# A local-attention and gated-product kernel: weight parts split in fewer passes, and another order for the head

## The chip, the cores and the metric

One core of one Trainium2 chip runs the whole kernel. The metric is device time in microseconds, from the launch's first work to its last. Engines are called PE (TensorE), DVE (VectorE), ACT (ScalarE), POOL (GpSimd) and SP (SyncE, which here only issues transfers).

## The reference, cut to what matters

Batch 4, 8 heads, 768 tokens, head size 64. A query attends to the tokens less than 16 away and to 24 block summaries (of keys the maximum over 32 tokens, of values the mean). The attention's output, 3072 tokens by 512, goes through two weight matrices of 512 by 1536, whose results are multiplied, and a third of 1536 by 512.

```
k_sum = k.reshape(B, H, nb, 32, D).max(axis=3);  v_sum = v.reshape(B, H, nb, 32, D).mean(axis=3)
scores_l = where(|i - j| < 16, scale * q @ k.T, -1e9);  scores_s = scale * q @ k_sum.T + log(32)
a = softmax(concat(scores_l, scores_s));  x = a @ concat(v, v_sum)
a = x @ w_a;  b = x @ w_b;  out = (a * b) @ w_out
```

The weights reach the kernel as numbers of 64 bits, two 32-bit words each.

## The kernel before, in words

**Tiles.** A tile is 128 tokens of a batch, all heads. Chunks `u` are of two tiles in batch 0 and three in the others. The scores of a tile are 120 columns for each of four head pairs and two halves `h` (96 neighbouring keys and 24 summaries), 480 columns for a half, in one PSUM bank.

**The first two chunks** (tiles 0 to 3 of batch 0, `first_attention`) have code of their own. `first_keys` loads six blocks of 128 keys (one token a partition, a run of 256 bytes for each head), turns each with four PE transposes (L507), copies it in two pieces to `kT` (L565, L566, ACT) and takes the block maxima (L573, DVE). A query tile is loaded and turned in the same way (L507), and ACT copies it with the factor 0.125 (L973). In `scores`, PE first writes the mask into the bank, as two parts in the reduced format fp32r multiplied by an identity (L695), and adds the 32 passes of scores (L708). DVE takes the maximum (L745) from the bank, ACT the exponentials with their sums (L759), DVE adds 1e-9 (L768), takes the reciprocal (L779) and makes from it diagonal matrices (L786). `transposes` multiplies by these (L807), which divides and transposes in one step; ACT copies the result (L819). `values` multiplies by the values (L856), after which ACT (L876) and DVE (L880) split the result in a high and a low part, `x`. The values of a tile come by `load_values` in three pieces, and the block means by six blocks of two tokens a partition, a POOL addition (L1000) and twelve PE passes (L991). Later chunks put the mask on with a DVE pass (L737) and divide on POOL (L794).

**Weights.** The three matrices are cut in 36 parts of 524 KB (a, b and o for each of 12 blocks `f`; part `i` is 0 to 35 in the order a0, b0, o0, a1, ...). `load_part` brings one, `convert(j)` splits parts 2j and 2j+1 in a high and a low part in fp32r. For a half (one part) ACT rescales the high words into bank `c0` (L424), DVE shifts (L432), DVE masks the exponent into bank `c1` (L439), DVE multiplies the low words by it (L445); ACT rounds to the high part (L477), POOL subtracts it (L482) and adds the low words' share (L488). From j = 3 on, the last steps take both halves at once. Loads for j > 3 wait until `convert(j - 4)` has read its words.

**The expert matmuls.** An item is a chunk (or both first chunks) with a block `f`: `up` (L1110, 12 matmuls for a and 12 for b), ACT and DVE make the product and split it (L1184 to L1192, L1214 to L1222), `down` (L1232). An item of one of the first chunks needs that chunk's `x` of both tiles, and the high and low words of its parts.

**What sets the order.** Every operation is added to a list (`Work`) with its engine, a rank, an estimated duration, and what it reads and writes. `emit` issues them engine by engine; for as long as `ORDER` has numbers for an engine, that engine's instructions come in exactly this order (a number is the place in the list). Each engine works through its instructions in order, so one that waits holds up all behind it; this holds for the transfers that SP issues. `SPIN` are matmuls without use that keep PE busy in the first 40 us.

## Time and profile before

| what | us |
|---|---|
| median of 3 runs (658.7 to 659.53) | 659.19 |
| span of the profiled execution, first to last instruction | 656.9 |
| median less that span | 2.3 |
| busy: PE / DVE / ACT / POOL | 647.7 / 409.9 / 250.8 / 187.8 |
| first expert matmul (L1110) starts | 38.33 |

The profiled execution has no time of its own beside its span; the difference to the runs' median stands for what lies around it. In the lists of instructions a row has start, length of the run of equal instructions, engine, line, operation, output and inputs, count, and in brackets idle time and what ended it. "PE" rows are matmuls, whose ends are modelled; "PEld" are weight loads. A plain fp32 matmul is two rows, one for each pass.

### The profile page before, as it was taken

The numbers are of one execution on the slowest core, as the hardware profiler recorded it, in microseconds if no ns is written. First come the engines' busy times: TensorE is split into PE (matmuls) and PEld (weight loads), VectorE is DVE, ScalarE is ACT, GpSimd is POOL, SyncE is SP. The second block draws the span as 40 slices with busy tenths as digits, with TensorE's granted clock in tenths as the row PEclk, the third lists the DMA queues.
The fourth block names the chain that finished last, engine by engine and source line by source line (L and its number), as shares of the span: only waits on it lengthen the run. The fifth ranks groups of instructions, "written<-read, shape, count | busy, mean of one in ns | idle before, by whom it ended". The sixth has DMA issues, their size and how long they took to land.

```text
span 656.9 us, 12984 instructions
## 1 busy us (share of the span) xinstructions
PE 647.7 (99%) x4943; PEld 599.3 (91%) x4943; DVE 409.9 (62%) x857; ACT 250.8 (38%) x749; POOL 187.8 (29%) x246
## 2 busy tenths in 40 slices
PE   8899999999999999999999999999999999999997
PEld 6699888899989999999999999999999999999997
DVE  3899999997786784666767846667652531122212
ACT  4997676523443441433333313343321411121111
POOL 6498999847333440111010101110100100000000
PEclk9999999999999999999999999999999999999999
DMA  9998666353443443322112422221100200010001
GB/s 218 277 286 243 229 188 173 79 118 105 128 92 78 112 95 57 71 82 44 39 39 52 84 42 43 41 82 35 25 1 1 71 1 1 0 49 1 0 1 49
DMA packets 158198, 54.71 MB, mean 83 GB/s; under 512 B 135736, under 2 KB 151352, under 8 KB 158136
## 3 DMA queue, kind: packets, MB, share of 16 engines
q1 hardware_dynamic: 157992, 53.75, 33.9%
q8 instruction: 39, 0.64, 0.4%
q14 instruction: 23, 0.19, 0.1%
q10 hardware_dynamic: 144, 0.13, 0.1%
HBM read 47.41 MB, written 6.44 MB: 82 GB/s over the span
## 4 chain that ended last, share of the span: by engine, by line
PE 89%; DMA 6%; SPq 2%; ACT 1%; issue 1%; POOL 0%; DVE 0%; DVEq 0%
PE h L1110 54%; PE o L1232 27%; PE c L708 3%; PE o L856 3%; SPq L357 2%; DMA raw<-in_moe_w_out_dram 1%; DMA space<-in_v_dram 1%; DMA raw<-in_moe_w_b_dram 1%; DMA raw<-in_moe_w_a_dram 1%; DMA space<-in_q_dram 1%; DMA qin<-in_q_dram 1%; SPq L389 1%; PE c L1110 1%; POOL space L482 0%; PE c L856 0%
## 5 line engine op out<-in xcount | busy, mean ns | idle before, releaser
L1110 PE MATMUL h<-x,w 128*128 128x384 f32 (+2 forms) x2064 | 389.1, 321 | 0.0
L1110 PEld LDWEIGHTS h<-x,w 128*128 128x128 f32 x2064 | 331.3, 190 | 10.5 <-issue 0.6
L1232 PE MATMUL o<-w,gh 128*128 128x512 f32 x534 | 131.7, 382 | 0.0
L1217 DVE TENSOR_TENSOR h<-h,g 128x384 f32<-128x384 f32 x71 | 40.2, 566 | 136.4 <-PE h L1110 128.8
L1219 ACT CAST gh<-h 128x384 fp32r<-128x384 f32 x71 | 34.0, 478 | 204.6 <-DVE h L1217 202.0
L1232 PEld LDWEIGHTS o<-w,gh 128*128 128x128 f32 x534 | 97.6, 189 | 12.2 <-issue 1.6
L840 DVE STREAM_TRANSPOSE pt<-s 32x256 f32<-32x256 f32 x228 | 99.4, 436 | 13.0 <-POOL s L794 8.3
L794 POOL TENSOR_TENSOR s<-s,nml 128x480 f32<-128x480 f32 x40 | 39.4, 987 | 220.2 <-DVE nml L779 218.1
L1110 PE MATMUL h<-late,w 128*128 128x384 f32 x288 | 93.9, 326 | 0.0
L759 ACT ACTIVATE s<-s,nml 128x120 f32<-128x120 f32 x160 | 61.3, 386 | 38.0 <-DVE nml L745 37.8
L1232 PE MATMUL o<-w,gl 128*128 128x512 f32 x231 | 63.3, 381 | 0.0
L1110 PEld LDWEIGHTS h<-late,w 128*128 128x128 f32 x288 | 54.4, 189 | 0.9
L1222 DVE TENSOR_TENSOR gl<-h,gh 128x384 fp32r<-128x384 f32 x71 | 39.4, 555 | 23.0 <-ACT gh L1219 22.5
L1214 ACT COPY g<-h 128x384 f32<-128x384 f32 x71 | 34.0, 478 | 51.3 <-PE h L1110 50.9
L1232 PEld LDWEIGHTS o<-w,gl 128*128 128x128 f32 x231 | 43.3, 189 | 6.5 <-issue 0.5
L639 POOL TENSOR_TENSOR S<-S 96x256 f32<-96x256 f32 (+3 forms) x58 | 33.0, 571 | 43.8 <-DMA S<-in_v_dram 41.1
L737 DVE SCALAR_TENSOR_TENSOR s<-c,mask 128x480 f32<-128x480 f32 x40 | 25.8, 652 | 24.0 <-PE c L708 23.9
L424 ACT ACTIVATE c<-raw 128x512 f32<-128x512 f32 x36 | 29.3, 814 | 13.2 <-DVE S L432 5.7
L759 ACT ACTIVATION_READ_ACCUMULATOR s<-s,nml 128x1 f32 x160 | 30.2, 189 | 0.0
L482 POOL TENSOR_TENSOR space<-space,w 128x1024 f32<-128x1024 f32 (+1 forms) x14 | 26.7, 1912 | 3.5 <-ACT w L477 3.2
L488 POOL TENSOR_TENSOR w<-space 128x1024 fp32r<-128x1024 f32 (+1 forms) x14 | 26.7, 1912 | 0.9
L745 DVE TENSOR_REDUCE nml<-s 128x4 f32<-128x480 f32 x40 | 25.8, 648 | 0.7
(139 smaller groups left out, 586.0 us busy)
## 6 DMA issues: line engine op xcount, KB each, us to landing
raw<-in_moe_w_a_dram SPq DMA_DIRECT2D x12, 512.0 KB, 5.7
raw<-in_moe_w_b_dram SPq DMA_DIRECT2D x12, 512.0 KB, 7.9
raw<-in_moe_w_out_dram SPq DMA_DIRECT2D x12, 512.0 KB, 4.8
out_dram<-S SPq DMA_DIRECT2D x23, 256.0 KB, 2.2
qin<-in_q_dram SPq DMA_DIRECT2D x288, 16.0 KB, 1.7
S<-in_v_dram SPq DMA_DIRECT2D x24, 192.0 KB, 3.3
kin<-in_k_dram SPq DMA_DIRECT2D x38, 100.0 KB, 2.5
vw<-in_v_dram SPq DMA_DIRECT2D x18, 192.0 KB, 3.4
```

The costliest lines, as they stand in the source:

```text
L424: nc.scalar.activation(bank["c0"], high[:, :, 1].bitcast(F32), AF.Prelu, scale=2.0**-112, alpha=-(2.0**32))
L482: lambda ms=ms, f8=f8: nc.gpsimd.tensor_tensor(out=f8, in0=f8, in1=parted(0)[:, ms].bitcast(F32), op=ALU.subtract),
L639: lambda: nc.gpsimd.tensor_tensor(out=out, in0=i0, in1=i1, op=ALU.add),
L759: lambda h=h, c=c, sums=sums: nc.scalar.activation(s[h][:, c, :], x[h][:, c, :], AF.Exp, bias=m[:, 0, h, c : c + 1], scale=1.0, accum_out= ...
L794: lambda h=h, r=r: nc.gpsimd.tensor_tensor(out=s[h], in0=s[h], in1=r[:, :, None].broadcast_to([P, NP, KN]), op=ALU.mult,),
L840: lambda js=js, qs=qs, rs=rs: nc.vector.transpose(out=pv[js, rs, qs], in_=sv[qs, rs, js]),
L1110: nc.tensor.matmul(ps, w[:, c, part, :], (xt[:, 4 * xpart : 4 * xpart + 4] if both else inputs_of(u, xpart))[:, :, c].rearrange("p g (a b) ...
L1214: act(CHAIN, 0.13 + W / 1030, [ak], gk, lambda: nc.scalar.copy(out=g, in_=pa))
L1217: lambda: nc.vector.tensor_tensor(out=pb, in0=pb, in1=g, op=ALU.mult),
L1219: act(CHAIN, 0.16 + W / 1030, [bk], [ghk], lambda: nc.scalar.copy(out=gh, in_=pb))
L1222: lambda: nc.vector.tensor_tensor(out=gl, in0=pb, in1=gh.bitcast(F32), op=ALU.subtract),
L1232: nc.tensor.matmul(bank[ok[j]], (gh if first else gl)[:, j * P : (j + 1) * P], w[:, :, part, :].rearrange("p (z a) n -> p z n a", a=2), st ...
```

## The change

*Weights.* A half takes one pass of ACT (rescaled high words, straight to SBUF), one of DVE for the low words (`tail`: times 2^-29, at most 7, as an integer into bank `c0` or `c1` by half), and one of DVE (`join`: shift by 3 and or). The product has the low bits in place, so that POOL's one subtraction gives the low part. For j < 3 each half has tiles of its own.

```
-            bank["c0"], high[:, :, 1].bitcast(F32), AF.Prelu, scale=2.0**-112, alpha=-(2.0**32)
...
-                    out=f.bitcast(I32), in0=e.bitcast(I32), scalar1=3, scalar2=None,
-                    op0=ALU.logical_shift_left,
...
-                    out=s.bitcast(I32), in0=f.bitcast(I32), scalar1=-(1 << 23), scalar2=None,
-                    op0=ALU.bitwise_and,
...
-                    out=p, in0=low.bitcast(U32), scalar=2.0**-52, in1=s, op0=ALU.mult, op1=ALU.mult
+            def scale(f=f, words=words):
+                nc.scalar.activation(
+                    f, words()[:, :, 1].bitcast(F32), AF.Prelu, scale=2.0**-112, alpha=-(2.0**32)
+                )
+            def tail(t=t, words=words):
+                nc.vector.tensor_scalar(
+                    out=t, in0=words()[:, :, 0].bitcast(U32), scalar1=2.0**-29, scalar2=7.0,
+                    op0=ALU.mult, op1=ALU.min,
+                )
+            def join(f=f, t=t):
+                nc.vector.scalar_tensor_tensor(
+                    out=f.bitcast(I32), in0=f.bitcast(I32), scalar=3, in1=t,
+                    op0=ALU.logical_shift_left, op1=ALU.bitwise_or,
+                )
...
             pool(
-                rank + 0.1 * hs[0], takes, hi, f,
...
-                    out=f8, in0=f8, in1=parted(0)[:, ms].bitcast(F32), op=ALU.subtract
...
-                    out=parted(1)[:, ms], in0=f8, in1=p8, op=ALU.add
+                rank + 0.1 * hs[0], 0.2 + 1.1 * len(hs), hi + f, lo,
+                lambda hs=hs, f8=f8: nc.gpsimd.tensor_tensor(
+                    out=parted(1, hs), in0=f8, in1=parted(0, hs).bitcast(F32), op=ALU.subtract
+                ),
             )
```

*Keys and queries of the first chunks.* A load takes four heads and 256 tokens, two tokens a partition (runs of 512 bytes); still six loads of keys and four of queries, of 262 KB each. Eight matmuls of 64 columns of weights by the identity turn one, the halves `h` into the two column halves of PE. ACT's copies pick the tokens up alternately; the queries of a chunk are turned together (`turn_queries`) and copied in four half pieces without the factor. The key maxima wait for PE alone.

```
+    def paired(x):
+        return x.rearrange("h (p t) d -> p h (t d)", t=2)
+    def turn_pairs(bk, x):
+        v4 = x.rearrange("p (h t d) -> p h t d", t=2, d=D)
+        for c in range(2):
+            for t in range(2):
+                n = 2 * c + t
+                for h in range(2):
+                    nc.tensor.matmul(
+                        bank[bk][h * D : (h + 1) * D, n * P : (n + 1) * P],
+                        v4[:, 2 * c + h, t, :], ident, start=True, stop=True,
+                        tile_position=(0, h * D),
+                    )
```

*Masks and division.* The mask matmuls and the three POOL instructions that make their inputs go. The first chunks have the DVE pass that the others have, and DVE multiplies by the reciprocal before four plain transposes.

```
-        if masked:
-            pe(rank + 0.1, 0.96, MK, banks, masks)
...
-                    lambda h=h, r=r, d=d: nc.vector.tensor_tensor(
-                        out=d[:, h], in0=ident[:, None, :].broadcast_to([P, NP, P]),
-                        in1=r[:, :, None].broadcast_to([P, NP, P]), op=ALU.mult,
+                    lambda h=h, r=r: nc.vector.tensor_tensor(
+                        out=s[h], in0=s[h], in1=r[:, :, None].broadcast_to([P, NP, KN]),
+                        op=ALU.mult,
...
-                    nc.tensor.matmul(
-                        bank[banks[h]][:KN, c * P : (c + 1) * P], s[h][:, c, :KN], d[:, h, c, :],
-                        start=True, stop=True,
+                    nc.tensor.transpose(
+                        bank[banks[h]][:KN, c * P : (c + 1) * P], s[h][:, c, :KN], ident
                     )
```

*Order.* `ORDER` and the banks of `SPIN` are new (its sixteen sizes are the same), and `ORDER` now ends about where the first two chunks' items end; behind that, ranks decide. Ranks of the first weight loads and value loads are earlier. The beginnings, with the numbers translated:

- SP: key blocks 1, 0, 2, 3, query half 1, key blocks 5, 4, query half 0; part 1; the six value blocks; two pieces of tile 0's values; part 0; their third piece; part 3; the queries of tiles 2 and 3; part 2; tile 1's values; part 4; a piece of tile 2's values; part 5; another; part 11; two pieces of values; part 7; values; part 9; values; parts 6, 13, 12, 8, 15, 10. (Before: eight loads; part 0; three value blocks, a query load; part 1; ...; tile 0's values behind part 5.)
- PE: five `SPIN`; turns of key blocks 1, 0, 2, 3, query half 1, keys 5, 4, query half 0, with one `SPIN` between; two `SPIN`; scores of tile 0; two; scores of tile 1; the means; two; transposes and product of tile 0; half of tile 1's transposes; the second queries; scores of tile 2; the other half; three `SPIN`; product of tile 1; scores of tile 3; the `up` of items 0 and 1; transposes and products of tiles 2 and 3; one `SPIN`; the `down` of item 0. (Before: scores of tiles 2 and 3 and six halves of transposes stand ahead of the first `up`, with the products of tiles 0 and 1 behind the scores of tile 3.)
- ACT: copies of key blocks 0, 2, 1, 5, a query quarter, 3, 4, two quarters; scale of part 1; a quarter; round part 1; exponentials of tile 0 and of half of tile 1; two copies of means; two copies of transposes; one exponential; scales of parts 0 and 3; split of tile 0; the other exponentials of tile 1; ...
- DVE: six key maxima; tail and join of part 1; masks and maxima of tile 0, of half of tile 1; divisions between; tail of part 0, tail and join of part 3; ...

More of the change, by code (lines that the diff above doesn't have):

```diff
@@ L383, in fn @@
         def fn():
-            if j not in raws:
-                raws[j] = wp.tile([P, 2048], I32, tag=f"W{j}", name=f"raw{j}")
-            dst = raws[j][:, i % 2 * 1024 : (i % 2 + 1) * 1024]
+            dst = raw(i)
             if nm != "o":
@@ L449, in convert @@
-        for n, h in [(n, h) for h in range(2) for n in range(3)]:
-            f, p, e, s, r = [fk[h]], [pk[h]], ["c0"], ["c1"], [rk[h]]
-            if n == 0:
-                act(CHAIN, 0.52, r, e, lambda h=h: scale(h))
-            reads, writes = ((e, f), (f, s), (r + s, p + [f"done{j}"] + r))[n]
-            dve(rank, 0.6, reads, writes, lambda n=n, h=h: step(n, h))
-        def parted(part):
-            if j not in homes:
-                homes[j] = wp.tile([P, 8, 2, P], F32R, tag=f"W{j}", name=f"w{j}")
-            return homes[j][:, :, part, :]
+        whole = [f"whole{j}"] if single and j > 2 else []
@@ new lines, in convert @@
+        for h in range(2):
+            f, t = fx[h], bank[f"c{h}"].bitcast(I32)
+            words = lambda h=h: raw(2 * j + h).rearrange("p (n t) -> p n t", t=2)
+            def scale(f=f, words=words):
[12 more added lines that the diff above has]
+                )
+            act(rank - 0.05, 0.66, [rk[h]], [fk[h], f"whole{j}.{h}"], scale)
+            dve(rank, 0.6, [rk[h]], [f"c{h}", f"done{j}.{h}"], tail)
+            dve(rank, 0.6, [f"c{h}"], [fk[h]], join)
@@ L461, in convert, with parted @@
+        work.add("-", 0, 0, 0, [f"done{j}.{h}" for h in range(2)], [f"done{j}"], lambda: None)
+        if whole:
+            work.add(
+                "-", 0, 0, 0, [f"{x}{j}.{h}" for x in ("whole", "done") for h in range(2)], whole, lambda: None
+            )
+        def parted(part, hs):
+            y = home(2 * j + hs[0])
+            if len(hs) == 2:
+                y = both[j]
+            return y[:, :, part, :]
         for hs in spans:
-            ms = slice(4 * hs[0], 4 * (hs[-1] + 1))
@@ L687, in scores @@
         m, mk = nml[t % 2], f"nml{t % 2}"
-        masked = u < FILL
-        def masks():
-            for h in range(2):
-                for part in range(2):
-                    nc.tensor.matmul(
-                        bank[banks[h]].rearrange("p (c x) -> p c x", x=P)[:, :, :KN], identr,
-                        maskr[part][:, kind, None, :KN].broadcast_to([P, NP, KN]),
-                        start=(part == 0), stop=False,
-                    )
+        first = u < FILL
         def fn():
@@ L728, in scores @@
         s = [t[:, :, :KN] for t in s]
[L729 to L730 removed]
+        x, xk = s, sk
         for h in range(2):
@@ L733, in scores @@
                 rank = rank_of(u, t) - 0.1 + 0.02 * h
[L734 to L742 removed]
+            dve(
+                rank, 0.6, [banks[h]], [sk[h], *(f"{sk[h]}{c}" for c in range(NP) if first)],
+                lambda h=h: nc.vector.scalar_tensor_tensor(
+                    out=s[h], in0=y[h],
+                    scalar=0.125, in1=mask[:, kind, None, :KN].broadcast_to([P, NP, KN]),
+                    op0=ALU.mult, op1=ALU.add,
+                ),
+            )
             dve(
@@ L752, in scores @@
             l = m[:, 1, h, :]
-            sums, r = l, x[h][:, :, 0] if masked else l
+            sums, r = l, y[h][:, :, 0] if first else l
             for c in range(NP):
@@ L902, in first_attention @@
         first_keys()
-        for takes, fn in (
-            (0.3, lambda: nc.gpsimd.tensor_copy(out=identr, in_=ident)),
-            (0.45, lambda: nc.gpsimd.tensor_copy(out=maskr[0], in_=mask[:, :2, :])),
-            (0.6, lambda: nc.gpsimd.tensor_tensor(
-                out=maskr[1], in0=mask[:, :2, :], in1=maskr[0].bitcast(F32), op=ALU.subtract
-            )),
-        ):
-            pool(-1, takes, [], MK, fn)
         q0, qk = spot(3)
```

266 lines of the change are left out of this document (119 added, 147 removed), and 54 rows, old and new, of the table ORDER.

## The prediction

> **What bounds the kernel now.** I read the page first, then TensorE's (PE) instructions in order of time, then the groups by line, then stretches of time for the transfers. The page:
>
> ```profile
> span 656.9 us, 12984 instructions
> PE 647.7 (99%) x4943; PEld 599.3 (91%) x4943; DVE 409.9 (62%) x857; ACT 250.8 (38%) x749; POOL 187.8 (29%) x246
> ...
> PE   8899999999999999999999999999999999999997
> ```
>
> The instructions of PE in order of time (start, length of the run of equal instructions):
>
> ```profile
> 1.43 2.50 PE L1338 MATMUL h<-ident 128*128 128x512 f32 x4 [1.43 <-POOL ident masks.py:199]
> 4.03 1.12 PE L507 MATMUL o<-ident,space 128*128 128x128 f32 x4
> ...
> 6.61 1.09 PE L507 MATMUL c<-ident,space 128*128 128x128 f32 x4
> 7.50 1.13 PE L1338 MATMUL h<-ident 128*128 128x256 f32 x4
> ...
> 9.78 0.60 PE L507 MATMUL c<-ident,space 128*128 128x128 f32 x4
> 10.21 0.64 PE L507 MATMUL o<-ident,space 128*128 128x128 f32 x4
> ...
> 12.73 0.60 PE L507 MATMUL h<-ident,space 128*128 128x128 f32 x4
> 13.10 1.12 PE L695 MATMUL o<-space 128*128 128x480 f32 x4
> 14.14 1.05 PE L708 MATMUL o<-kT,qT 64*64 64x120 f32 x32
> 15.01 1.00 PE L708 MATMUL o<-kT,space 64*64 64x120 f32 x32
> ...
> 34.09 1.15 PE L856 MATMUL h<-pt,vw 120*64 120x64 f32 x32
> 35.07 1.10 PE L856 MATMUL h<-space,space 120*64 120x64 f32 x32
> 36.40 1.98 PE L807 MATMUL o<-pt,s 128*120 128x128 f32 x16 [0.23 <-DVE pt L786]
> 38.33 2.92 PE L1110 MATMUL h<-x,w 128*128 128x256 f32 x24
> 41.09 1.04 PE L807 MATMUL o<-space,space 128*120 128x128 f32 x8
> ...
> 47.89 1.15 PE L856 MATMUL o<-space,space 120*64 120x64 f32 x32
> 48.98 0.70 PE L1232 MATMUL o<-w,gl 128*128 128x512 f32 x2
> ```
>
> The stretch from 80 to 100 us (columns: stretch, its length, busy time and instructions of PE, weight loads, VectorE, ScalarE, GpSimd, then clock, DMA, GB/s):
>
> ```profile
> 80.00:100.00 20.00, 20.00 (x94) 17.51 (x93) 19.19 (x33) 15.53 (x28) 19.09 (x10) 1.00 0.58 156
> ```
>
> From 38.33 PE never waits noticeably: 94 matmuls of 512 columns in 20 us are 0.213 us each, which is the rate at which the columns stream, and that in a stretch where VectorE and GpSimd are 95% busy. So what the change saves on those two is worth nothing by itself there. The time is: the point at which the expert matmuls (L1110) start, plus work that the change leaves alone. Only the head, up to about 49 us, can pay. In it PE waits for a chain through ScalarE (ACT), VectorE (DVE) and the loads.
>
> **The parts, with their prices.** Groups by line (count, then busy time and mean ns of one):
>
> ```profile
> L759 ACT ACTIVATE s<-s,nml 128x120 f32<-128x120 f32 x160 | 61.3, 386 | 38.0 <-DVE nml L745 37.8
> L737 DVE SCALAR_TENSOR_TENSOR s<-c,mask 128x480 f32<-128x480 f32 x40 | 25.8, 652 | 24.0 <-PE c L708 23.9
> L745 DVE TENSOR_REDUCE nml<-o 128x4 f32<-128x480 f32 x8 | 4.9, 646 | 0.0
> L432 DVE TENSOR_SCALAR space<-c 128x512 int32<-128x512 int32 x22 | 15.0, 682 | 2.6 <-ACT c L424 2.6
> L439 DVE TENSOR_SCALAR c<-space 128x512 int32<-128x512 int32 x22 | 15.1, 684 | 0.2
> L445 DVE SCALAR_TENSOR_TENSOR space<-raw,c 128x512 f32<-128x512 uint32 x22 | 16.8, 762 | 0.1
> L424 ACT ACTIVATE c<-raw 128x512 f32<-128x512 f32 x36 | 29.3, 814 | 13.2 <-DVE S L432 5.7 <-DVE space L432 4.2 <-DVE s L737 3.0
> L482 POOL TENSOR_TENSOR space<-space,w 128x1024 f32<-128x1024 f32 (+1 forms) x14 | 26.7, 1912 | 3.5 <-ACT w L477 3.2
> L786 DVE TENSOR_TENSOR space<-ident,o 128x512 f32<-128x512 f32 x4 | 2.7, 678 | 0.0
> L768 DVE TENSOR_SCALAR o<-nml 128x4 f32<-128x4 f32 x8 | 1.2, 159 | 1.6 <-ACT s L759 1.3 <-ACT space L759 0.3
> L477 ACT CAST w<-space 128x512 fp32r<-128x512 f32 x6 | 3.7, 630 | 0.0
> L819 ACT COPY space<-o 120x512 f32<-120x512 f32 x4 | 2.4, 597 | 0.5 <-PE o L807 0.5
> ```
>
> *Weights.* A half part loses one of three DVE passes (L432, L439, L445: 0.68+0.68+0.76 = 2.13 us) and one of two GpSimd passes (L482 and its like). Neither new pass is in the trace. The tail pass reads the same strided words as L445 and the join reads SBUF and PSUM at once as L445 does: between 0.68 (L439) and 0.81 (ScalarE's strided pass L424), I take 0.76 for both. 36 halves save 36 x (2.13-1.52) = 22 us of DVE (20 to 28 by the bounds), all under PE's cover after 38 us. In the head, six halves save 4 us on an engine that is full there.
>
> *Masks.* 16 mask matmuls (four at 13.10 end where scores start at 14.14: about 1 us a tile) leave PE. DVE gets eight passes of 0.65 (L737), and its eight diagonal builds (L786, 0.68) become eight divisions of like size. Maxima and exponentials stay, so the head's DVE gains 5.2 us and loses 4: it is no lighter, only the order differs. The scale of 0.125 moves from the query copies into the mask pass, at no instruction; the key maxima no longer wait for the key copies, which frees an engine that has nothing else to do then.
>
> *Transposes.* Scaled ones are eight matmul passes of about 0.11 us a half tile (16 in the 1.93 us from 36.40 to 38.33), plain ones four (10.21 less 9.78: 0.43 us). The paired turns are 16 passes of 64 columns of weights. If the two halves of the columns run side by side, as in L856 (32 passes from 34.09 to 35.07, 0.031 each, against 0.055 for 64 columns one after another), a turn costs 16 x 0.054 = 0.87 against 0.43 now.
>
> *Loads.* Stretches with 256-byte runs only, with mostly 512-byte runs, and with mostly 1 KB runs (the last column counts):
>
> ```profile
> 6.00:9.00 3.00, 2.63 (x13) 2.17 (x11) 1.27 (x2) 1.85 (x6) 2.40 (x14) 1.00 1.35 218
> 14.00:15.00 1.00, 1.00 (x33) 0.86 (x36) 0.06 (x1) 0.64 (x1) 0.00 (x0) 1.00 1.23 291
> 23.00:25.00 2.00, 2.00 (x17) 1.72 (x17) 1.65 (x6) 1.63 (x7) 0.94 (x2) 1.00 1.10 347
> 30.00:35.00 5.00, 4.13 (x73) 3.06 (x73) 4.96 (x12) 4.95 (x22) 4.86 (x5) 1.00 0.74 154
> ```
>
> Two tokens a partition make runs of 512 bytes: 262 KB take 0.90 us and not 1.20. The first key comes at about 3.7 (4.03 less 0.3), the eighth load at 10.0, where the last query was turned at 12.73 before. With the new order of SP behind it, at these rates: part 1 at 11.6 (524 KB at 347: 1.5), the six value blocks by 17.6, tile 0's values (360 KB in 256-byte runs) at 20.8 behind part 0, the second queries at 24 behind part 3, tile 1's values (393 KB) at 27.3 behind part 2, part 4 at 28.9.
>
> **The walk through the head**, each engine in its written order. Five warm-up matmuls of 1,024 columns together stand where 640 took 2.50: PE is free at about 5.1. The first turn is at half rate (four transposes from 6.61 to 7.50 are 0.22 each, those from 9.78 to 10.21 0.11), 1.8; the second straddles the release near 7.5 and ends at 8.2. ScalarE then paces:
>
> ```profile
> 7.74 0.42 ACT L565 COPY kT<-c 128x320 f32<-128x320 f32 x1 [0.56 <-PE c L507]
> ...
> 8.27 0.45 ACT L565 COPY kT<-o 128x320 f32<-128x320 f32 x1
> ```
>
> A key's two copies repeat every 0.53. Three run to 10.3; the turn of key block 5 needs the bank that the third frees and ends at 11.6; ScalarE waits that long (it is next in its order), then copies three keys and four query halves (0.3, the same rows by their columns) in 2.6. Scores of tile 0 start at 14.4 (14.14 before). No gain yet; the masks' microseconds are eaten by the dearer turns.
>
> DVE: the join of part 1 stands ahead of tile 0's first mask and waits for ScalarE's pass at 14.9; it ends at 15.7, so it costs 0.1. This wait is new: behind it stand all of DVE's masks, and behind those the exponentials, tile 0's transposes and its product; each 0.1 more here is 0.1 there. Then mask and maximum of each half at 0.62 apiece: maxima at 17.0, 18.2, and 19.4 (tile 1). ScalarE does four exponentials in 1.35 (L759's 386 ns overlap a little): done at 18.4, 19.8, 21.1; the mean copies to 22.2. Divisions (sum and reciprocal at 0.16 like L768, and 0.65) end at 21.9; four plain transposes 0.43 a half, two copies of 0.6 (L819) to 23.3; tile 0's product runs 23.5 to 24.5, ten microseconds ahead of 34.09, because its values now come early in SP's order. The second queries turn to 27.2; tile 1's last half is divided at 27.8; scores of tile 2 run 28 to 29, that half is transposed by 29.4. ScalarE first has one scale and three casts of parts (0.62 each, L477: 27.9 to 30.4), then its copy (30.9). Tile 1's product 31.1 to 32.1, scores of tile 3 behind it, its split copy done at 33.05. Part 0's low words: GpSimd 30.5 to 31.8, in time. **The first expert matmul: 33.15 against 38.33.**
>
> Then 48 expert matmuls in 5.4 (38.33 to 41.09 is 2.76 for 24) to 38.6, part 4 converted at 35.8 just ahead of its use. Four transposes and two products are 1.7+2.1, with 0.35 of waiting: 42.8. The same work ends before at 48.98 less one down block of four (4 x 0.216): 48.1. Gain 5.3 us. Next late would be part 6 (needed 51.6, GpSimd done 50.9): covered by 0.7 us only.
>
> Sum: span 656.9-5.3 = 651.6. The median 659.19 is 2.3 above the profiled span, which is what lies around it: **653.9**. With 0.75 a key copy and 0.1 more at each hop the start is 35.1 with 1.3 of waiting behind: gain 2.9, 656.3. With new passes at 0.68 and the turn of block 5 unblocked: gain about 6.5.
>
> **The clock.** The turns at 4.03 and 6.61 show half rate although PE is busy from 1.43. If five matmuls in one block, and turns that are matmuls rather than transposes, release the clock by 5.1, two turns get 1.9 us cheaper, loads allow 1.4 of it: gain 6.7, 652.5. The Trainium skill ("TensorE: Matmul & The Clock Gate", Part 1: The HAM clock gate) says that about 3.4 us of sustained work in a free-running window releases it, which would be this case. By that rule the trace should have been fast before 6.61; it was not, so the row decides the forecast.
>
> **Rivals.** *Slower: parts starve PE.* In SP's written order three loads wait for conversions (part 11 for parts 2 and 3; part 13 for 4 and 5, about 41; part 15 for 6 and 7, about 45.4), and parts 12, 8 and 10 queue behind them; part 10's scale pass then stands ahead of part 8's on ScalarE. At 347 GB/s part 10 lands at 50 and parts 8 and 9 are ready at 57, used at 58.5. At the 154 GB/s of 30 to 35 us, it lands at 58, PE stands 7 to 8 us: 653.9+8 = 662. It decides from 1.5 us of delay on. For: three waits in a row; against: that low rate went with runs of 256 bytes, these are 1 KB and more. *No pairing of the turns:* 1.74 each, scores at 20.1, nearly all lost: 659.7. Against: L856. *Slow chain:* 656.3, above. *Early clock:* 652.5, above.
>
> **How the numbers follow.** Forecast 653.9: 0.45; early clock 652.5: 0.20; slow chain 656.3: 0.20; no pairing 659.7: 0.06; starved 662: 0.09. 0.2% is 1.3 us, about what a measurement of this kernel tells from no change, so faster is below 657.9. The first three are faster but for a sliver: 0.82; same 0.09, slower 0.09. The range 650.8 to 658.2 takes in the bounds of the three (gain 8.4 if early clock and cheap passes come together) and leaves out the last two.
>
> **What would show it.** Scores of tile 0 near 14.4; product of tile 0 near 24 with no DMA as releaser; first L1110-like matmul of 256 columns near 33; no gap over 0.5 us on PE behind 43; DVE's two passes at 0.76 and GpSimd's busy time near 160; a turn 0.87. Wrong: the start after 36, PE gaps of microseconds between 50 and 65 released by POOL or ACT behind a raw load, or turns of 1.7.

## The result, and the profile after

The changed kernel took 666.13 us (median of 4 runs, 663.16 to 668.94), the kernel before beside it 659.15: a ratio of 1.0106 (95% interval 1.0072 to 1.0139). It is slower by 1%, where 653.9, faster by 0.8%, was forecast. The profiled execution took 667.64 us, with a span of 665.9. Its page:

```profile
span 665.9 us, 13031 instructions
...
PE 647.9 (97%) x5015; PEld 598.5 (90%) x5015; DVE 395.6 (59%) x829; ACT 252.0 (38%) x753; POOL 143.1 (21%) x218
```

VectorE and GpSimd are 14 and 45 us less busy than before, PE is as busy as before, and the span is 9.0 us longer: the time went into waits of PE. Its instructions in order of time (start, length of the run of equal instructions, and in brackets the wait ahead of it and what ended it), first the head:

```profile
7.69 1.92 PE L530 MATMUL o<-ident,space 128*64 128x128 f32 x32
...
15.34 1.05 PE L688 MATMUL o<-kT,qT 64*64 64x120 f32 x32 [0.76 <-ACT qT L937]
...
24.91 1.15 PE L829 MATMUL h<-pt,vw 120*64 120x64 f32 x32 [1.55 <-ACT pt L792]
...
34.80 5.62 PE L1081 MATMUL h<-x,w 128*128 128x256 f32 x48 [0.67 <-ACT x L849]
...
43.56 0.29 PE L829 MATMUL o<-space,space 120*64 120x64 f32 x4
45.69 1.04 PE L829 MATMUL o<-space,space 120*64 120x64 f32 x28 [1.84 <-DMA space<-in_v_dram]
...
47.10 2.05 PE L1203 MATMUL o<-w,gh 128*128 128x512 f32 x4
...
65.44 2.86 PE L1081 MATMUL h<-x,w 128*128 128x512 f32 x12 [0.92 <-ACT g L1130]
...
112.44 0.42 PE L688 MATMUL c<-kT,qT 64*64 64x120 f32 x4 [1.55 <-DVE S L425]
...
178.72 1.67 PE L1203 MATMUL o<-w,x 128*128 128x512 f32 x6 [1.32 <-ACT x L1160]
...
184.25 1.03 PE L829 MATMUL o<-pt,vw 120*64 120x64 f32 x28 [0.92 <-DVE pt L813]
...
200.36 1.03 PE L829 MATMUL o<-pt,vw 120*64 120x64 f32 x28 [0.92 <-DVE pt L813]
```

The head does come earlier: the first expert matmul starts at 34.80 and not at 38.33. Behind it are waits that the kernel before does not have. I counted the columns of the expert matmuls as they start, and took for the same count the time here less the time before. At points in time of the kernel before this lag is about -5.8 us at 44 us (some of this only because two `up` stand ahead of the attention of tiles 2 and 3 here), +0.3 at 56, +2.4 at 100, +4.7 at 124, +9.0 from 200 us to the end. So about 3 us of gain were lost four times over:

**A, 43 to 50 us.** Tile 3's product waits 1.84 us for its last block of values. Then the clock halves (stretch, length, busy time and instructions of PE, weight loads, VectorE, ScalarE, GpSimd, clock, DMA, GB/s):

```profile
43.20:46.60 3.40, 1.56 (x51) 1.41 (x46) 2.06 (x4) 1.21 (x4) 0.00 (x0) 1.00 1.10 313
46.60:50.00 3.40, 3.40 (x14) 2.81 (x10) 2.58 (x5) 2.73 (x6) 0.93 (x1) 0.50 1.07 369
```

The four `down` matmuls at 47.10 take 2.05 us at that clock, and such a stretch costs 1.7 us (half of its 3.41).

**B, 60 to 100 us.** The wait at 65.44 is for a copy on ScalarE. ScalarE's own rows show why it is late, and VectorE's beside it:

```profile
52.85 0.37 ACT L1155 COPY g<-h 128x256 f32<-128x256 f32 x1 [2.71 <-PE h L1081]
...
54.34 0.81 ACT L414 ACTIVATE space<-raw 128x512 f32<-128x512 f32 x1
55.53 0.37 ACT L1155 COPY g<-h 128x256 f32<-128x256 f32 x1 [0.38 <-PE h L1081]
55.80 3.15 ACT L414 ACTIVATE space<-raw 128x512 f32<-128x512 f32 x4
```

```profile
59.04 0.69 DVE L425 SCALAR_TENSOR_TENSOR space<-space,c 128x512 int32<-128x512 int32 x1 [1.75 <-issue]
...
110.18 1.42 DVE L419 TENSOR_SCALAR c<-raw 128x512 int32<-128x512 uint32 x2 [2.15 <-DMA raw<-in_moe_w_out_dram]
111.70 0.69 DVE L425 SCALAR_TENSOR_TENSOR S<-S,c 128x512 int32<-128x512 int32 x1
```

By the written order the four scales from 55.80 on are of parts 12, 10, 13 and 8, and the join at 59.04 is part 8's: VectorE had done part 8's tail by 55.02, and stood from 57.29 until its scale came as the last of the four (it ended at 58.95; the `issue` in the row names no releaser). All of this stood, besides, behind a copy (52.85) that waited 2.71 us for PE. The casts of parts 8 and 9 end at 61.7 here, 51.4 before; of 14 and 15 at 72.8 and 66.0.

**C, 112 us.** The scores of tile 5 write banks `c0` and `c1`, which the tails and joins of parts 34 and 35 hold until 112.4 and 113.0. VectorE's list has part 35's tail first of these four, and that part's load has landed only at 110.2 (VectorE's rows above).

**D, 172 to 200 us.** The written order has ended (at about 145 us; in the kernel before at about 225). By rank GpSimd does a division of the softmax (L768) behind a sum of values (L628) that waits 4.89 us for its load. VectorE's transposes (L813) wait for that division, and PE's products wait for them. The gate product that VectorE has behind the first of these transposes comes late too, and with it the `x` of 178.72:

```profile
173.99 0.72 POOL L628 TENSOR_TENSOR S<-S 96x256 f32<-96x256 f32 x1 [4.89 <-DMA S<-in_v_dram]
174.68 0.99 POOL L768 TENSOR_TENSOR s<-s,nml 128x480 f32<-128x480 f32 x1
...
177.06 0.88 DVE L813 STREAM_TRANSPOSE pt<-s 32x256 f32<-32x256 f32 x2 [4.75 <-POOL s L768]
```

### The profile page after: what moved, and what is told of

Same layout as the page of the kernel before. It is cut to its first block, busy times and chain, and to the rows that moved or that the text cites. A ratio compares the mean times of both kernels' runs of the same rounds, so it can differ in the third digit from the quotient of the medians.

```text
span 665.9 us, 13031 instructions
## 1 busy us (share of the span) xinstructions
PE 647.9 (97%) x5015; PEld 598.5 (90%) x5015; DVE 395.6 (59%) x829; ACT 252.0 (38%) x753; POOL 143.1 (21%) x218
## 4 chain that ended last, share of the span: by engine, by line
PE 77%; DVE 5%; SPq 4%; DMA 2%; issue 1%; POOL 1%; ACT 0%; DVEq 0%; POOLq 0%; ACTq 0%
PE h L1081 46%; PE o L1203 25%; SPq L322 4%; PE o L829 3%; PE c L688 3%; DMA raw<-in_moe_w_out_dram 2%; DVE pt L813 2%; DVE S L813 1%; DVE c L419 1%; PE c L1081 1%; DMA qin<-in_q_dram 0%; DMA S<-in_v_dram 0%; PE c L829 0%; DVE space L425 0%; DVE S L425 0%
## 5 line engine op out<-in xcount | busy, mean ns | idle before, releaser
L1203 PE MATMUL o<-w,gh 128*128 128x512 f32 x534 | 133.8, 385 | 0.9 <-ACT gh L1135 0.7
L813 DVE STREAM_TRANSPOSE pt<-s 32x256 f32<-32x256 f32 x228 | 99.3, 436 | 18.7 <-POOL s L768 14.7
L768 POOL TENSOR_TENSOR s<-s,nml 128x480 f32<-128x480 f32 x40 | 39.4, 988 | 221.5 <-DVE nml L755 217.7
L735 ACT ACTIVATE s<-s,nml 128x120 f32<-128x120 f32 x176 | 67.6, 387 | 37.3 <-DVE nml L721 37.1
L628 POOL TENSOR_TENSOR S<-S 96x256 f32<-96x256 f32 (+3 forms) x58 | 33.2, 572 | 54.2 <-DMA S<-in_v_dram 50.2
L459 POOL TENSOR_TENSOR w<-space,w 128x1024 fp32r<-128x1024 f32 (+1 forms) x14 | 26.7, 1914 | 35.0 <-ACT w L455 24.3
L735 ACT ACTIVATION_READ_ACCUMULATOR s<-s,nml 128x1 f32 x176 | 33.5, 190 | 0.0
L419 DVE TENSOR_SCALAR c<-raw 128x512 int32<-128x512 uint32 x36 | 27.9, 789 | 3.2 <-DMA raw<-in_moe_w_out_dram 2.2
L721 DVE TENSOR_REDUCE nml<-s 128x4 f32<-128x480 f32 x44 | 28.4, 647 | 0.7
L1203 PE MATMUL o<-w,x 128*128 128x512 f32 x96 | 26.3, 388 | 1.4 <-ACT x L1160 1.3
```

The source lines that it names most:

```text
L419: nc.vector.tensor_scalar(out=t, in0=words()[:, :, 0].bitcast(U32), scalar1=2.0**-29, scalar2=7.0, op0=ALU.mult, op1=ALU.min,)
L628: lambda: nc.gpsimd.tensor_tensor(out=out, in0=i0, in1=i1, op=ALU.add),
L721: lambda h=h: nc.vector.tensor_reduce(out=m[:, 0, h, :], in_=x[h], axis=AX.X, op=ALU.max, negate=True),
L735: lambda h=h, c=c, sums=sums: nc.scalar.activation(s[h][:, c, :], x[h][:, c, :], AF.Exp, bias=m[:, 0, h, c : c + 1], scale=1.0, accum_out= ...
L768: lambda h=h, r=r: nc.gpsimd.tensor_tensor(out=s[h], in0=s[h], in1=r[:, :, None].broadcast_to([P, NP, KN]), op=ALU.mult,),
L813: lambda js=js, qs=qs, rs=rs: nc.vector.transpose(out=pv[js, rs, qs], in_=sv[qs, rs, js]),
```

## The experiments

The theory was that operations and their durations are as predicted and that the written order loses the time at A to D; the rival, that the work itself or the loads bind, so that a wait removed comes back elsewhere. No run but the fourth (two more matmuls without use) and the seventh (the new conversion in the old kernel) differs from its parent in an operation. Ratios are to the kernel before, run beside each. Edits are cut to the entries that change, and the breaks of their lines are not the file's.

| run | us (lowest to highest) | ratio, 95% interval |
|---|---|---|
| e1_values_earlier (A) | 666.86 (664.04 to 668.48) | 1.0116, 1.0082 to 1.0149 |
| e2_order_carried_on (D) | 665.63 (664.32 to 666.29) | 1.0095, 1.0080 to 1.0110 |
| e3_before_short_order | 667.62 (666.11 to 667.94) | 1.0123, 1.0108 to 1.0138 |
| e4_spins_in_the_gap | 665.42 (664.23 to 668.51) | 1.0101, 1.0075 to 1.0127 |
| e5_scores_later | 673.14 (667.60 to 674.91) | 1.0192, 1.0137 to 1.0246 |
| e6_parts_earlier | 665.51 (664.73 to 666.08) | 1.0091, 1.0076 to 1.0106 |
| e7_before_new_parts | 658.31 (657.89 to 660.03) | 0.9987, 0.9978 to 0.9996 |
| e8_all_four | 670.72 (669.79 to 671.88) | 1.0172, 1.0156 to 1.0188 |
| e9_parts_in_turn (A, B) | 666.30 (664.79 to 668.16) | 1.0101, 1.0076 to 1.0127 |
| e10_in_turn_carried_on (A, B, D) | 662.25 (659.41 to 664.68) | 1.0040, 1.0023 to 1.0057 |
| e11_last_parts_earlier (A, B, C, D) | 657.82 (657.31 to 658.77) | 0.9970, 0.9959 to 0.9981 |
| e12_work_in_the_gap | 659.47 (658.78 to 660.21) | 0.9999, 0.9988 to 1.0009 |
| e13_both | 658.66 (657.92 to 659.53) | 0.9986, 0.9977 to 0.9996 |
| e14_without_values (B, C, D) | 658.74 (657.62 to 660.14) | 0.9991, 0.9982 to 1.0001 |
| e15_without_turn (A, C, D) | 658.93 (657.79 to 660.22) | 0.9995, 0.9985 to 1.0004 |
| e16_without_tail (A, B, C) | 661.22 (659.67 to 663.05) | 1.0027, 1.0015 to 1.0039 |

**One place at a time.** e1_values_earlier, on SP (154 and 155 are value pieces of tile 3):

```
-        198 119 258 156 121 234 154 246 155 233
+        198 119 258 156 154 155 121 234 246 233
```

> The changed kernel with one edit: the two last load pieces of tile 3's value blocks stand right behind the first one on SP, ahead of two query loads and two weight parts. Theory A (tile 3's product waits 1.84 us for its last piece, and the clock halves for 3.41 us behind that gap, which costs 1.7 more): no wait of over 0.5 us at tile 3's product, the clock stays at full speed from 5.7 us on, the time falls by about 3.5 us from the changed kernel's 666.1, to 662 to 663. Rival (the pieces are late because the queue is full of bytes, whatever their place): the wait moves to the query blocks or to a weight part, the second product of the first experts waits as long, and the time stays within 1 us of 666. Rival (the halving is not due to the gap): the wait goes, the clock still halves once, and the time falls by 1.8.

The wait and the halved clock at 43 to 50 us went, and with them 3.8 us by 52 us. But PE now stood longer some 60 us later, for ScalarE's rounding to `gh`. In ScalarE's list it is behind the scale of part 34, which waited 2.31 us for its load until 106.47. The clock halved there:

```profile
108.55 1.62 PE L1203 MATMUL o<-w,gh 128*128 128x512 f32 x4 [2.25 <-ACT gh L1135]
110.10 2.25 PE L688 MATMUL c<-kT,qT 64*64 64x120 f32 x32
```

The scores at 110.10 take 2.25 us and not 1.05. The theory was right at its place and wrong on the time; the first rival had the time (within 1 us of 666) and a weight part as the next to be late, but at the first experts and not 60 us later.

e2_order_carried_on (the first line of PE's list that goes on; its other lines and the other engines' lists go on likewise):

```
-        628 624 626 648 625 645 633 627
+        628 624 626 648 625 645 633 627 653 634 654 906 907 914 912 913 759 921 919 920 928 926
```

> The changed kernel with its written order carried on behind its end by the order of the kernel before, for the same operations (PE from 123 to 193 entries, POOL from 60 to 153 and so on); nothing before 127 us is touched. Theory D (from about 127 to 200 us ranks decide the order, POOL puts the division of a tile behind value sums that wait 4.9 us for their loads, and PE waits for the weights of the division): PE's waits of 0.9 to 1.3 us at 177, 183, 194 and 200 us are gone, and the time falls by 4 to 4.5 us from 666.1, to about 662. Rival (these waits come from the lag that the kernel already has there, or from the clock): they stay or move on, and the time stays within 1.5 us of 666.

D's waits went: from 168 us to the end the trace gains some 3.5 us on the changed kernel. The time gained 0.5, in the profiled run because its clock halved at A and at C, where that of the changed kernel had halved at A alone. e3_before_short_order shortens the lists of the kernel before in the same way (PE's again, the others likewise):

```
-        652 673 653 649 651 662 660 658 661 682 659 667 679 687 668 688 940 941 948 946 947 793
...
+        652 673 653 649 651 662 660 658 661 682 659 667 679
```

> The kernel before with its written order cut where that of the changed kernel ends (PE 127, ACT 169, DVE 253, POOL 92 and SP 154 entries are kept); no operation is changed. Theory D: the shorter order alone costs the kernel before about 4 us, between 130 and 200 us, at the same lines (transposes and products behind POOL's division): 663 to 664. Rival (the ranks give the kernel before as good an order as its list, and the changed kernel loses there through its new conversion or its lag): within 1 us of 659.2.

It costs the old kernel 8.4 us, twice what was expected. Between 196 and 212 us the profiled run loses some 6, with a halved clock behind this wait:

```profile
199.53 2.08 PE L1208 MATMUL o<-w,gh 128*128 128x512 f32 x4 [2.15 <-ACT gh L1165]
```

The row of PE has another line than in D, but the chain behind it is D's: GpSimd's sums of values waited 6.33 us for a load, a division stood behind them, and VectorE's transposes waited for that division:

```profile
196.82 1.78 DVE L816 STREAM_TRANSPOSE pt<-s 32x256 f32<-32x256 f32 x4 [5.09 <-POOL s L770]
```

About 2 us are lost by 70 us already, where nothing was changed (a wait of 0.58 us for values at 49.02 is one of them); why, this run does not show. So ranks do cost time where lists end, in either kernel.

e4_spins_in_the_gap, two matmuls without use of 512 columns ahead of tile 3's product:

```
-        178 176 183 185 180 187 2607
+        178 176 183 185 180 2620 2621 187 2607
...
+    ("o1", 512), ("o1", 512),
```

> The changed kernel with two plain matmuls of 512 columns into a bank that is free, right ahead of tile 3's product, where PE waits 1.84 us for the last value piece. The wait itself stays. Theory (the gap, with the transposes ahead of it, halves the clock): the clock stays at full speed behind 5.7 us, and the time falls by the price of the halving, 1.7 us a time, to about 664.4, with less spread between runs than the 663.2 to 668.9 of the changed kernel. Rival (the halving has another cause, the load of the matmuls or chance): it shows in the same share of the runs, and the time stays at 666 or is up to 0.3 above.

```profile
43.20:46.60 3.40, 3.40 (x47) 2.03 (x43) 2.06 (x4) 1.03 (x4) 0.00 (x0) 1.00 1.12 355
46.60:50.00 3.40, 3.40 (x27) 3.24 (x27) 2.73 (x5) 2.90 (x6) 0.86 (x1) 1.00 1.05 362
```

With the gap filled the clock stays up here, so the gap is what halves it. This execution's clock halved later, at C, behind 2.0 us of waiting, and it took 668.51 us. The other three runs have a mean clock of 0.999 and took 664.23 to 665.70, near the forecast of 664.4, but the changed kernel's two runs with that clock took 663.16 and 664.62. So the time, 0.7 us less at the median, does not show the gain.

e5_scores_later (476 are the scores of tile 5):

```
-        584 586 589 585 598 587 594 476 599 595-597 608
+        584 586 589 585 598 587 594 599 595-597 476 608
```

> The changed kernel with one entry moved: on PE the scores of tile 5 stand behind the rest of item (1,7) and the up product of item (1,8), about 4.6 us of matmuls later. Theory C (PE stood 1.55 us there only because those scores write banks c0 and c1, which the tail and join of part 35 hold, and part 35's load lands at about 110): the wait at the scores is gone or under 0.4 us, no other wait takes its place, and the time falls by 1.5 to 2, and by up to 1.7 more in the runs whose clock halved behind that wait: 662 to 664.5. Rival (a late part reaches PE by more than one way: ScalarE's copies of the next item stand behind the same part's conversion): a wait of 1 us or more for gh or g at L1135 or L1130 within 108 to 114 us takes its place, and the time stays within 1 us of 666.

The time rose by 7 us, where the rival said that it would stay, and the waits are not for `gh` or `g` but for VectorE's `x`:

```profile
110.69 4.34 PE L1081 MATMUL h<-x,w 128*128 128x512 f32 x12 [2.55 <-DVE x L1138]
...
123.52 4.54 PE L1081 MATMUL h<-x,w 128*128 128x512 f32 x12 [3.00 <-DVE x L1138]
```

VectorE's list still had part 35's join ahead of the `x` of 110.69, and then the transposes of the next keys, which overwrite what those scores read: it stood 6.47 us for the scores, until 117.19, with its next products behind. One engine's list was moved and the others' were not. e6_parts_earlier moves loads on SP alone:

```
-        198 119 258 156 121 234 154 246 155 233 270 269 245 282 257 310 332
+        198 119 258 156 121 234 154 246 155 233 270 269 245 282 257 310 309 321 332
...
-        393 405 334 746 742 404 417 416 808 805 803 751 431 432
+        393 405 334 404 417 416 746 742 431 432 808 805 803 751
```

> The changed kernel with only SP's order edited behind 46 us: loads of parts 16, 18, 26, 28 to 35 are moved ahead of query-block loads, above all ahead of the two (numbers 746 and 808) at which SP stands 6.1 and 5.1 us. Theory B/C (the parts are late because they queue behind query blocks and SP's own waits): parts 34 and 35 are issued 4 us or more earlier than 102.5 and 103.4, PE's waits at 64, 100 and 110 us shrink from 0.9, 0.5 and 1.6 us to under 0.5 each, and the time falls by 2.5 to 4 from 666.1, to about 662.5 to 663.5. Rival (a part can be loaded only when VectorE and GpSimd are done with the space it takes, so the place on SP is not the limit): SP waits at the parts instead, their conversions come no earlier, and the time stays within 1 us.

Parts 16 and 18 were issued at 47.4 and 48.1 and not at 59.6 and 66.7, and their scales ran at 67.9 and 74.5, not at 68.1 and 74.8: the loads were not what held them; that the lists of ScalarE and VectorE were, e9 shows. Part 34 was issued at 102.7 as before, its space not being free earlier. That part of the theory was wrong.

**The conversion alone**, e7_before_new_parts, in the kernel before:

```
-        for n, h in [(n, h) for h in range(2) for n in range(3)]:
+        for h in range(2):
...
+            act(CHAIN, 0.52, [rk[h]], [fk[h], f"whole{j}.{h}"], scale)
+            dve(rank, 0.6, [rk[h]], [f"c{h}", f"done{j}.{h}"], tail)
+            dve(rank, 0.6, [f"c{h}"], [fk[h]], join)
```

> The kernel before with the new conversion of the weight parts alone (tail and join instead of shift, mask and product; one GpSimd pass instead of two), in the order of before: each new pass takes the place of the old one that it replaces. Nothing else of the change is in it. Theory (PE bounds this kernel from 38.3 us on and the parts are ready in time; the passes are off the path, and the loss is in the order): within 1.0 us of 659.2, with VectorE some 20 us and GpSimd some 40 us less busy. Rival (the new conversion itself loses, by its use of both banks or by freeing the parts' space in another order): 661 or more.

```profile
PE 647.4 (99%) x4943; PEld 600.0 (91%) x4943; DVE 390.2 (59%) x821; ACT 249.7 (38%) x749; POOL 144.3 (22%) x221
```

VectorE is 20 us and GpSimd 44 us less busy than before, and the kernel gains 0.8 us, as the theory had it. The new passes lose nothing.

**Repairs together.** e8_all_four holds the edits of e1, e2 and e6, and a later place for the scores than e5's:

```
-        584 586 589 585 598 587 594 476 599 595-597 608 609
+        584 586 589 585 598 587 594 599 595-597 608 476 609
```

> The changed kernel with all four repairs of the order: the value pieces of tile 3 first (A), the parts ahead of the query blocks (B), the scores of tile 5 some 8 us of matmuls later (C), and the written order carried on by that of before (D). No operation is changed. Theory (the 5.8 us of the head are real and were given back at these four places, and the clock halves only behind gaps of about 2 us): the lag behind the kernel before stays at minus 4 to minus 6 us from 44 us to the end, the clock stays at full speed from 5.7 us on, and the time is 653.5 to 656, below the 659.2 of before. Rival (each place only passes its wait on to the next, since loads come at the times that the DMA queue sets): 658 to 662, with new waits of 1 us or more between 60 and 130 us.

The later scores sank it. VectorE waits for them with all that it has behind, and PE then waits 5.8 us for VectorE:

```profile
119.83 0.78 DVE L614 STREAM_TRANSPOSE kT<-kin 128x576 f32<-128x576 f32 x1 [7.58 <-PE c L712]
```

e9_parts_in_turn leaves the scores alone, keeps e1's edit, and puts the conversions in the order of use (ScalarE; VectorE's list likewise, and parts 14, 16 and 18 earlier on SP):

```
-        525 242 527 250 532 271 259 274 247 286 534 262 254 266 283 540 542 278
+        242 525 250 247 527 532 259 262 254 534 271 274 266 286 283 540 278 542
```

> The changed kernel with the value pieces of tile 3 first on SP (as in the run that did this alone) and with the weight parts 8 to 19 converted in the order in which the experts use them: on ScalarE and VectorE the steps of parts 8 and 9 stand ahead of those of 10 to 13 and ahead of the copies of the next items, and on SP parts 14, 16, 18 and 19 are loaded ahead of the later query blocks. No operation is changed. Theory E (the losses between 48 and 113 us have one root: VectorE stands 2.9 us at the join of part 8, whose scale ScalarE does only behind the scales of parts 12, 10 and 13 and behind copies that wait for PE, and all later conversions inherit this): the casts of parts 8 to 15 end 5 us or more earlier than the 61.7 to 72.8 of the changed kernel, PE's waits at 61 to 64 and at 106 to 112 us (1.2 and 2.4 us) shrink under 0.5 each, the clock stays at full speed, and the time falls to 660 to 662. Rival (the conversions are bound by the loads, whose bytes the DMA queues bring no faster): the casts move by less than 2 us, a wait of over 1 us stays in 60 to 66 us, and the time is 664 or more.

```profile
50.03 1.50 ACT L414 ACTIVATE space<-raw 128x512 f32<-128x512 f32 x2
...
53.23 1.66 ACT L414 ACTIVATE space<-raw 128x512 f32<-128x512 f32 x2 [0.71 <-DMA raw<-in_moe_w_b_dram]
54.79 1.03 ACT L455 CAST w<-space 128x1024 fp32r<-128x1024 f32 x1
```

Now parts 9 and 8 are scaled from 50.03, their cast ends at 55.8 (61.7 in the changed kernel), that of parts 14 and 15 at 65.8 (72.8), and PE has no wait at 60 to 66 us: B is shown. PE is 2.1 us ahead of the kernel before at 100 us, where the changed kernel is 2.4 behind. C was not mended by it, though theory E had said so: PE waited 1.50 there, the clock halved behind it, and D's waits took the rest. e10_in_turn_carried_on adds e2's longer lists:

> The same kernel with, besides, the written order carried on by that of the kernel before, as in the run that did this alone (there PE's waits between 172 and 200 us went, worth 4.4 us by the two traces, though a second halving of the clock hid it in the time). Theory E with D: both gains stand, the time is 655.5 to 658, below the 659.2 of before. Rival (D's waits are replaced by others as soon as PE comes earlier): within 1.5 us of the run without the longer order.

D is worth 4.05 us here, and 662.25 is still over the forecast 655.5 to 658. What is left is C, now with the clock halved for two stretches on end (6.8 us):

```profile
108.07 2.47 PE L712 MATMUL c<-kT,qT 64*64 64x120 f32 x32 [1.55 <-DVE S L449]
```

**C, in two ways**, both on e10. e11_last_parts_earlier, on SP (446, 447, 461 and 462 are parts 32 to 35):

```
-        663 660 753 756 750 755 748 749 446 757 812 447 807 744 799 461 813 462
+        663 660 446 447 753 756 750 755 748 749 461 462 757 812 807 744 799 813
```

> The run with parts in turn and the order carried on (662.25), and on SP the loads of parts 32 to 35 ahead of query blocks of later chunks: part 34 and 35 are issued 1.3 to 2 us earlier and have fewer bytes ahead of them. Theory C (the scores of tile 5 wait for banks c0 and c1, which the last part's tail and join hold until its load has landed): the wait of 1.55 us at 108 us falls under 0.5, the clock does not halve there, and the time falls by 2 to 4, to 658.5 to 660. Rival (the space that part 34 and 35 are loaded into is free only at about 96.5 us, and the bytes take as long as before): the wait stays over 1 us and the time is 661.5 or more.

Part 35, issued at 97.7 and not 99.0, is cast by 107.4 and not 109.3; the wait is gone, the clock stays up from 6.29 us to the last matmul, and the kernel beats both others, by 1.4 us the kernel before. The gain on e10, 4.4 us, is more than theory C said. PE's rows from 46 to 240 us show two waits:

```profile
97.18 1.99 PE L1227 MATMUL o<-w,gh 128*128 128x512 f32 x8 [0.51 <-ACT gh L1159]
139.93 1.13 PE L1227 MATMUL o<-w,x 128*128 128x512 f32 x4 [0.61 <-ACT x L1184]
```

e12_work_in_the_gap (599 is an `up`, 593 VectorE's product that frees its bank; 464, 465 and 467, 468 are the tails and joins of parts 34 and 35):

```
-        584 586 589 585 598 587 594 476 599
+        584 586 589 585 598 587 594 599 476
...
-        453 591 467 464 465 468 593
+        453 591 464 465 593 467 468
```

> The run with parts in turn and the order carried on (662.25), with the gap at the scores of tile 5 filled: on PE the second up product of item (1,8), 2.8 us, stands ahead of those scores, and on VectorE the gate product of item (1,7), which frees its bank, and part 34's steps stand ahead of part 35's. The scores themselves come about 1 us later. Theory (1.6 us of wait and 3.4 us of half clock behind it are lost there, and useful work in the gap takes back both): no wait of over 0.5 us in 105 to 112 us, a clock at full speed from 6 us to the end, and 657.5 to 659.5. Rival (VectorE's next steps, the transposes of the next keys, stand behind those scores, so that later scores cost as much behind, as they did when the scores were moved by 4.6 us): a wait of 1 us or more between 110 and 120 us, and 661.5 or more.

```profile
106.48 1.13 PE L1227 MATMUL o<-w,gh 128*128 128x512 f32 x4 [1.74 <-ACT gh L1159]
...
116.97 2.86 PE L1105 MATMUL h<-x,w 128*128 128x512 f32 x12 [1.27 <-DVE x L1162]
```

Waits of 3.0 us in place of one of 1.55 (the rival had the one at 116.97, but not the time), and still 2.8 us faster than e10, since the clock did not halve: e10's own two runs with a mean clock of 0.999 or more took 659.41 and 659.83, as long as this kernel. So more than half of what C costs in e10 is the clock.

e13_both has e11's edit and e12's:

> Both of these edits. Theory: all four places mended, 656.5 to 658.5, below the 659.3 of before, with the clock at full speed throughout. Rival (what is left is not in the order: the parts come no faster than the DMA queues and VectorE bring them, and PE waits elsewhere as it gets earlier): 659.5 or more, with new waits between 85 and 150 us.

It is 0.8 us slower than e11, just over its forecast: once the part is early, the later scores only cost (1.27 us at 115).

**One repair taken out of e11**, each by the reverse of its diff: e14_without_values (A), e15_without_turn (B) and e16_without_tail (D), in this order:

> The mended kernel (657.82) with one repair taken back: the two last load pieces of tile 3's values stand again behind two query loads and two weight parts. If the places add up: PE waits 1.8 us at tile 3's product at 43 to 46 us, the clock halves for 3.4 us behind it, and the time is 3.2 us longer, about 661. If the mended order behind it has slack that takes the loss up: within 1 us of 657.8.

> The mended kernel with one repair taken back: the parts 8 to 19 are loaded and converted again in the order of the changed kernel, in which VectorE stands at part 8's join. If the places add up by the lags of the traces: waits of 1.2 us at 61 and 0.7 at 97 us and about 1.0 us more, 659. If the late conversions also make parts 34 and 35 late (their space is freed by part 27's conversion): the wait at the scores of tile 5 comes back too, with a halved clock, and the time is 661 to 663.

> The mended kernel with the written order ending again at about 127 us, ranks deciding from there. If theory D holds: the waits of 0.9 to 1.7 us at 172 to 200 us come back and the time is 3.7 to 4.5 us longer, 661.5 to 662.3. If the earlier PE or its undisturbed clock was what removed them: within 1 us of 657.8.

Their waits, one fence for each:

```profile
44.62 1.03 PE L853 MATMUL o<-space,space 120*64 120x64 f32 x28 [1.42 <-DMA space<-in_v_dram]
```

```profile
61.80 2.86 PE L1105 MATMUL h<-x,w 128*128 128x512 f32 x12 [0.91 <-ACT g L1154]
```

```profile
172.06 1.67 PE L1203 MATMUL o<-w,x 128*128 128x512 f32 x6 [1.34 <-ACT x L1160]
177.59 1.03 PE L829 MATMUL o<-pt,vw 120*64 120x64 f32 x28 [0.91 <-DVE pt L813]
```

So A is worth 0.9 us (the forecast for adding up was 3.2), B 1.1, C 4.4 (e10 against e11) and D 3.4. They add up to 9.8, while all four are worth 8.3. The waits come back where they were; in the traces of e14 to e16 the clock never halved behind them. A's wait is 1.42 us here and not 1.84, no halved stretch follows it, and what lies behind takes up part of it: so it costs 0.9, where the trace of the changed kernel had 3.5.

Single repairs showed nothing because C, later on, took up what they saved. In the traces of e1, e4 and e9 a halved clock at C is a part of that. It is not all: e1's one run with a mean clock of 0.999 took 664.04 us, no less than the changed kernel's two such runs (663.16 and 664.62).

## Why the prediction was wrong, point by point

- *Durations: right, but for GpSimd.* Tail 0.79 and join 0.68 us (0.76 for both forecast); two paired turns take 1.92 (0.87 each); the product of tile 0 starts at 24.91, no DMA ending its wait (24). GpSimd fell further than forecast, to 143 us busy and not 160. Smaller slips of the working change little: by its own rows 48 expert matmuls take 5.5 us and not 5.4, a scaled transposing pass 0.12 and not 0.11, the saving on VectorE is at least 18 us and not 20, and the runs of the changed kernel are 1.7 us longer than their spans, where 2.3 was added.
- *The head: right in kind, 3 us and not 5.3.* Scores of tile 0 at 15.34 (14.4), first expert matmul at 34.80 (33.15). Once both kernels have done the same work, the lead is about 3 (e11: 2.9 at 52 us). By the usual spacing of each kind of matmul PE has 2.7 us less to do (the masks and scaled transposes, less the dearer turns). What it stands beyond this spacing in its first 38 us is 10.3 us, and was 10.5: the walk expected the waits to shrink, and they did not.
- *The early clock* (a rival) is nearly there: sixteen passes take 1.09 us at 6.76. It brought nothing that can be seen: the start is 1.65 us later than the forecast without it. Nor is it shown that the new turns bring it: with the transposes of the old head full speed came at 7.70 us in the kernel before, but at 4.92 in e3 and 10.22 in e7.
- **The step that failed**: "From 38.33 PE never waits noticeably", carried over to the new kernel as "plus work that the change leaves alone", with "Next late would be part 6 [...] covered by 0.7 us only" and the rival of late parts as the only looks behind the head. That PE never waits was a property of the old written order, and the order is part of the change. The lists of all five engines behind the head are new: value pieces behind weight parts (A), part 8's scale behind three others (B), scores that need the last part's banks 9 us earlier (C), and lists that end at about 145 us, where the old ones went on to about 225 (D). B was thought of as a rival only, and A, C and D were not walked, though that the order ends earlier stood in the description of the change. The term that the sum put at nothing, PE's waits behind the head with the halved clock that follows them, measured about 12 us: from 3 ahead to 9.0 behind.
- *The rival "parts starve PE"* (0.09) named a step of B, "part 10's scale pass then stands ahead of part 8's on ScalarE". It put the delay down to late loads, where the order of the conversions was enough, and its size was off: 1.1 us (e15), and not 8. That its 662 is nearer to the measured time than the forecast is chance, since A, C and D are not in it.
- *"No gap over 0.5 us on PE behind 43"* was the line that would show it wrong, and it did.

What stays open: e11 gains 1.4 us on the kernel before, and the conversion alone (e7) 0.8; by difference the new head is worth some 0.6, even with its order mended. Of the 3 us of its head 1.9 are lost between 52 us and the end, 1.1 of them in the two waits shown under e11. Whether another order would keep them was not tried.

## What to carry to other kernels

Where an order is written out by hand, the order is the change: walk every queue as far as the new lists reach and past their end, and ask of each wait what stands behind it. A repair that saves nothing alone may still be needed, since the next late load takes up what it saves; take repairs out of the full set, one by one, to see their worth. And an entry moved in one engine's list can hold up the other engines, whose lists still expect it at its old place (e5, e8); loads alone could be moved here without such a loss (e1, e6, e11).

## What the runs showed of the hardware

The clock falls by stretches. Up to the last matmul it halved, in all traces, for 3.41 us or (twice) for 6.83, and began to do so at whole multiples of 3.413 us from where it had first come up (in the changed kernel full speed at 5.66, half at 46.62: 40.96 us, 12 times 3.413). I cut each run so, and summed PE's idle time in each stretch up to 230 us by the spacing of its matmuls. Eleven stretches at full speed held 2.27 us of idle time or more, and the clock halved behind each; behind the others it halved twice, both times at 43 us (2.12 and 1.86), and not behind three of 2.01 to 2.04. Such a sum depends on the spacing that one takes for short passes, by up to 0.2 us: for the 1.86 another choice gives 2.1. So the limit lies near 2 us of idle time in a stretch, and is not known more closely. A wait of 2 us therefore costs 2 us or 3.7, by where it falls.

This is part of the spread of the changed kernel: its runs of 663.2 and 664.6 us have a mean clock of 0.999, those of 667.6 and 668.9 of 0.996 and 0.994. By these means the two slower ones had one and two such stretches (the profiled 667.6 had one), which is 1.7 and 3.4 us of the 3.0 to 5.8; what the rest is, these runs do not show.

The Trainium skill ("TensorE: Matmul & The Clock Gate", Part 1: The HAM clock gate) has a window of 3,413 ns that runs freely, with which these traces agree: the stretches have that length, and full speed first comes at 4.3 to 10.2 us, by the run. With a window that runs freely, the prediction's "should have been fast before 6.61" does not follow: the first whole window behind 1.43 can end as late as 8.26 (an estimate from that page's 3,413 ns), and the kernel before had full speed at 7.70. e7, whose first matmuls are the same, had it at 10.22, which this does not explain. The Trainium skill's section "Why this matters for your kernels", on the same page, asks for no gaps of more than about 3 us; here one of 2.25 us (e1, at 108.55) was enough.
